# Gated linear attention before a mixture of experts: loads of a step issued singly, one product and one copy on other engines, state products ahead of the gate

## The chip, the cores and the metric

The kernel runs on one core of a Trainium2 chip. The metric is the device time of that core in microseconds (us), as the median of several executions. A core has five engines that run their own instruction streams and wait for each other through semaphores: TensorE (PE in the profile, with PEld for its weight loads), VectorE (DVE), ScalarE (ACT), GpSimd (POOL) and SyncE (SP). SyncE computes nothing here: it issues the DMAs between device memory and the on-chip memory, in the order of its stream. The profile also names queues: SPq is SyncE's.

## The reference

A recurrence over 768 positions for 4 batches and 8 heads of width 48, whose output is reshaped to 3072 tokens of width 384, followed by 8 experts with 384 tokens each:

```python
f = 1.0 / (1.0 + np.exp(-f_logit))
for t in range(S):
    state = f[:, :, t, :, None] * state + np.einsum('bhd,bhe->bhde', k[:, :, t], v[:, :, t])
    y[:, :, t] = np.einsum('bhd,bhde->bhe', q[:, :, t], state)
...
x = np.ascontiguousarray(attn_out.transpose(0, 2, 1, 3)).reshape(B * S, H * D)
logits = x @ w_gate
# pairs (token, expert) in falling order of logit; a token goes to the first expert with room
for e in range(E):
    mask = assigned == e
    h = np.maximum(x[mask] @ w1[e], 0.0)
    out[mask] = h @ w2[e]
```

All data are float32.

## The kernel before

The kernel has two parts, one behind the other on the same core. The first is the scan, which computes the recurrence and the gate's logits. The second finds the assignment of tokens to experts by a search (small VectorE and TensorE operations in alternation), gathers the tokens' rows from device memory, and runs the two matmuls of each expert. The change touches the scan alone.

The scan works on chunks of 128 positions of one batch with all 8 heads: 6 chunk positions times 4 batches are 24 chunks, numbered position first (`chunks`, line 357). A chunk goes through some thirty small functions, the stages. They are written out by hand as a tuple `stages` (line 358): each entry is a function and a number n, and step s calls the function on chunk s - n. So one step holds work of five chunks at different ages, and the tuple's order is the order of the instructions on every engine's stream; nothing is reordered later. `begun` is the order of the first three steps, -1 to 1 (line 363), `drain` and `finale` those of the last two. An entry `(None, 0)` is the place at which small jobs that prepare the search are put in ("extras" below).

What the stages do, by the names that the profile shows:

- `clamp` (line 164, GpSimd) and `decays` (169 and 170, ScalarE, two activations) turn the loaded `f` into the log-decay `g`.
- `cumulated` (174, TensorE) sums g over positions into the PSUM bank `L`; `clipped` (179, VectorE) reads it into `dl`; `powers` (185, ScalarE) makes `ek` and `eq`, exponentials of dl and of -dl.
- `scaled` (191) multiplies: `kg` = k * ek on GpSimd, `qg` = q * eq on VectorE.
- In the step after that, `turn_q` and `turn_k` (231, TensorE) transpose qg and kg into the two PSUM banks `T`; ScalarE copies them out (239). `products` (252, TensorE) multiplies kg with v for the new state, in a part of the PSUM bank `small`; `next_state` (263, VectorE) adds it to the faded old state `R`. `turned` (160, GpSimd) makes `w`, a copy of v's upper heads with the two halves of its positions exchanged. `scores` (273, TensorE) multiplies kT and qT.
- One step later, `masked0` and `masked1` (281, VectorE) copy the scores under the causal mask; `inner` (303) and `outer` (314), both TensorE, make the output in two PSUM banks `Y`.
- One step later still, `joined` adds the two banks (322 on ScalarE, then 323 on VectorE) into `yT`; `turn_y` (328, TensorE) transposes it into the first bank T; `copy_y` (334) copies it out as `x`, on VectorE for all but the last three chunks and on ScalarE for these; `gate` (344, TensorE) multiplies yT with the gate's weights `wg_rows` into columns of the bank L; `gated` (348, VectorE) takes the logits; `with_logits` (351, GpSimd) appends them to x; `store` (355, SyncE) writes x to device memory.
- `lengths` and `spanned` (204 on TensorE, 209 on VectorE), `faded` (217, ScalarE) and `kept_part` (223, GpSimd) make `R`; `gl` lies between (212, GpSimd).

The loads: `load` (line 141) is called at the head of step s for chunk s + 2 and puts four DMAs next to each other on SyncE's queue: q and k of that chunk, f of the chunk after it, and v. The tiles of f, k and q have 5 buffers each, v has 7 (`NV`). In front of the first step, chunks 0 and 1 are loaded in the same way; `load_gate` loads wg_rows at step 1.

The lines of the order that the change touches:

```python
(copy_k, 1), (cumulated, 0), (clipped, 0), (masked1, 2), (turn_y, 3), (copy_y, 3),
(gate, 3), (gated, 3), (decays, -1), (products, 1), (lengths, 0), (turned, 1),
(powers, 0), (scaled, 0), (spanned, 0), (next_state, 1), (faded, 0), (kept_part, 0),
```

Of the kernel before, what the change touches and what calls it, by code (L numbers as in the profile page):

```python
# [11 lines left out]
FP32 = mybir.dt.float32  # L12
# [3 lines left out]
ALU = mybir.AluOpType  # L16
# [9 lines left out]
def kernel(  # L26
# [11 lines left out]
    nc = tc.nc  # L38

    B, H, S, DH = q.shape  # L40
# [3 lines left out]
    C = 128  # L44
# [41 lines left out]
    work = attn.enter_context(tc.tile_pool(name="attn", bufs=2))  # L86

    def kept(shape, dtype, name):
        return work.tile(shape, dtype, name=name, tag=name, bufs=1)
# [6 lines left out]
    q_bufs = [kept([128, H, DP], FP32, f"qg{i}") for i in range(NB)]  # L96
    k_bufs = [kept([128, H, DP], FP32, f"kg{i}") for i in range(NB)]
    a_bufs = [kept([128, 2, HP, 128], FP32, f"am{i}") for i in range(NB)]
    NV = 7
    v_bufs = [kept([128, H, DP], FP32, f"v{i}") for i in range(NV)]  # L100
# [37 lines left out]

    state = {}

    def load(G):
        n = G["i"] + 1
        fetch(G, (("q", q), ("k", k)) if G["i"] else (("f", f_logit), ("k", k), ("q", q)))
        if n < len(chunks):
            fetch(chunks[n], (("f", f_logit),))
        fetch(G, (("v", v),))

    def fetch(G, parts):
        b, c = G["b"], G["c"]
        for nm, src in parts:  # L150
            t = v_bufs[G["i"] % NV] if nm == "v" else work.tile(
                [128, H, DH], FP32, name=nm, tag=nm, bufs=5)
            nc.sync.dma_start(
                out=t[:, :, 0:DH], in_=src[b, :, C * c:C * c + C, :].rearrange("h t d -> t h d"))
            G[nm] = t

    def turned(G):
        G["w"] = w = work.tile([128, H // 2, DP], FP32, name="w", tag="w", bufs=4)
# [27 lines left out]

    def scaled(G):
        i = G["i"] % NB
        for nm, t, src, e, eng in (("kg", k_bufs[i], "k", "ek", nc.gpsimd),
                                   ("qg", q_bufs[i], "q", "eq", nc.vector)):  # L190
            eng.tensor_tensor(out=t[:, :, 0:DH], in0=G[src][:], in1=G[e][:], op=ALU.mult)  # L191
            G[nm] = t


# [32 lines left out]
    def turn_of(nm, src):  # L227
        def turn(G):
            G[nm + "_ps"] = t = T[nm == "kT"]
            for hp in range(HP):  # L230
                nc.tensor.transpose(  # L231
                    out=t[:, 128 * hp:128 * hp + 128],
                    in_=G[src][:, 2 * hp:2 * hp + 2, :].rearrange("t h d -> t (h d)"),
                    identity=ident[:])

        def copy(G):
            G[nm] = work.tile([128, HP, 128], FP32, name=nm, tag=nm, bufs=3)
            to = G[nm][:].rearrange("p a t -> p (a t)")
            nc.scalar.copy(out=to, in_=G[nm + "_ps"][:])

        return turn, copy

    turn_k, copy_k = turn_of("kT", "kg")
# [86 lines left out]

    def copy_y(G):
        G["x"] = x = work.tile([128, DX], FP32, name="x", tag="x", bufs=5)
        copy = nc.scalar.copy if G["i"] + 3 >= len(chunks) else nc.vector.tensor_copy
        copy(
            out=x[:, 0:D].rearrange("t (a r b d) -> t a r b d", a=2, r=2, b=2),
            in_=G["X"][:].rearrange("t (a b r d) -> t a r b d", a=2, b=2, r=2)[:, :, :, :, 0:DH])

# [15 lines left out]
    def store(G):  # L353
# [2 lines left out]

    chunks = [{"b": b, "c": c, "i": c * B + b} for c in range(NCH) for b in range(B)]
    stages = ((clamp, -1), (masked0, 2), (joined, 3), (turn_q, 1), (copy_q, 1), (turn_k, 1),
              (copy_k, 1), (cumulated, 0), (clipped, 0), (masked1, 2), (turn_y, 3), (copy_y, 3),
              (gate, 3), (gated, 3), (decays, -1), (products, 1), (lengths, 0), (turned, 1),  # L360
              (powers, 0), (scaled, 0), (spanned, 0), (next_state, 1), (faded, 0), (kept_part, 0),
              (None, 0), (with_logits, 3), (scores, 1), (inner, 2), (outer, 2), (store, 3))
    begun = tuple(x for x in stages if x[1] >= 0) + ((clamp, -1), (decays, -1))
    drain = ((masked0, 2), (masked1, 2), (turn_q, 1), (joined, 3), (copy_q, 1), (turn_k, 1),
             (copy_k, 1), (turned, 1), (gate, 3), (gated, 3), (scores, 1), (None, 0), (turn_y, 3), (copy_y, 3),
             (inner, 2), (outer, 2), (masked0, 1), (masked1, 1), (None, 1), (with_logits, 3),
             (store, 3))
    finale = ((joined, 3), (inner, 2), (outer, 2), (None, 0), (gate, 3), (gated, 3), (turn_y, 3),
              (None, 1), (joined, 2), (copy_y, 3), (None, 2), (gate, 2), (gated, 2), (None, 3),
              (turn_y, 2), (copy_y, 2), (with_logits, 3), (store, 3), (with_logits, 2),  # L370
              (store, 2), (None, 4))
# [2 lines left out]
    def later(step, go, at=0):  # L374
        extras.setdefault((step, at), []).append(go)

    AHEAD = 2
    ALL = len(chunks) + 2

    def attention(first, last):  # L380
        for step in range(first, last):
            if AHEAD <= step + AHEAD < len(chunks):
                load(chunks[step + AHEAD])
            order = stages
            if step < 2:
                order = begun
            elif step > len(chunks):
                order = finale
            elif step == len(chunks):
                order = drain  # L390
            for stage, n in order:
                if stage is None:
                    for go in extras.pop((step, n), ()):
                        go()
                elif 0 <= step - n < len(chunks):
                    stage(chunks[step - n])
# [28 lines left out]
    def last_of(t, n):  # L425
        return t.unsqueeze(len(t.shape)).to_broadcast(tuple(t.shape) + (n,))
# [38 lines left out]
    for i in range(3):  # L465
        rows_ = slice(NQ * i // 3, NQ * (i + 1) // 3)
        later(11 + i, lambda r=rows_: nc.vector.tensor_copy(
            out=blocks[:, r], in_=last_of(linef[:, r], NT)))
# [84 lines left out]
    def load_weights(e, pool, slot, parts=(0, 1), behind=None):  # L553
        for part in parts:
            shape, src = (([128, DC, F], moe_w1), ([128, FC, D], moe_w2))[part]
            w = pool.tile(shape, FP32, name=f"w{part + 1}", tag=f"w{part + 1}_{slot}", bufs=1)
            if behind is not None:
                nc.scalar.copy(out=w[0:1, 0, 0:1], in_=behind)
            nc.sync.dma_start(out=w[:], in_=src[e].rearrange("(c p) f -> p c f", p=128))
            slots.setdefault(e, [None, None])[part] = w  # L560
# [29 lines left out]
    def load_gate():  # L590
# [9 lines left out]
        out=wg[:], in_=moe_w_gate.rearrange("(c p) e -> p c e", p=128)))  # L600
    later(0, lambda: idle_turns(5))
    with tc.manual_schedule(engines=FIXED):
        load(chunks[0])
        load(chunks[1])
        for z in range(2):
            nc.sync.dma_start(out=mask[HC * z:HC * z + HC, 1], in_=mask[HC - HC * z:C - HC * z, 0])
        attention(-1, LAST + 2)
        load_weights(0, early, 0)
        attention(LAST + 2, ALL)
        load_weights(1, early, 1)  # L610
# [765 lines left out]
    with tc.If(again > 0):  # L1376
# [7 lines left out]
        with tc.For_i(0, B, 1) as b:  # L1384
            x = pool.tile([128, NCH, D], FP32, name="xb", tag="xb", bufs=1)
            with tc.For_i(0, HP, 1) as hp:
                scan_pair(pool, x, b, hp)
            nc.sync.dma_start(
                out=xd[:, :].rearrange("(b c t) d -> b t c d", b=B, c=NCH)[
                    bass.ds(b, 1), :, :, 0:D].rearrange("b t c d -> (b t) c d"),  # L1390
                in_=x[:])
            for c in range(NCH):
                G = {"x": x[:, c, :]}
                X = ps("X", "T")
                for d in range(DC):
                    nc.tensor.transpose(out=X[:, 128 * d:128 * d + 128],
                                        in_=G["x"][:, 128 * d:128 * d + 128], identity=ident[:])
# [3 lines left out]
                for d in range(DC):  # L1401
# [3 lines left out]
                    out=logits[:, bass.ds(b * NCH + c, 1)].rearrange("p o e -> p (o e)"),  # L1405
                    in_=G["lg"])
# [30 lines left out]
```

## Time and profile before

| what | value |
|---|---|
| device time, median of 3 runs | 453.06 us (451.3 to 453.6) |
| the profiled execution | 454.26 us |
| its span in the profile | 452.5 us |
| mean granted TensorE clock | 0.981 |
| start of turn_q in steps 1 to 4 | 9.14, 14.20, 19.59, 25.55 us |
| start of turn_q in steps 5 to 9 | 30.93, 36.32, 42.49, 48.97, 56.01 us |
| start of turn_q in steps 12 to 15 | 73.49, 79.31, 85.15, 90.97 us |
| start of turn_q in steps 16 to 19 | 97.78, 104.77, 112.95, 119.37 us |
| start of turn_q in steps 21 to 23 | 131.02, 136.58, 142.25 us |
| first matmul of the experts | 179.5 us |

The span runs from the first to the last instruction of the profiled execution. The stretches from one turn_q to the next are the lengths of the steps: 5.8 us in the middle of the scan, more around 42 to 56 us and around 97 to 119 us. Busy times of the engines in four stretches, with the granted clock of TensorE and the share of time in which the DMA engines were busy:

```profile
core 0: us, PE busy (x) PEld busy (x) DVE busy (x) ACT busy (x) POOL busy (x), PEclk, DMA share, GB/s
31.00:41.80 10.80, 10.40 (x261) 9.01 (x261) 9.32 (x22) 7.27 (x16) 6.34 (x16) 1.00 0.95 206
79.30:85.10 5.80, 5.62 (x146) 4.78 (x142) 4.61 (x14) 3.61 (x8) 3.07 (x8) 1.00 0.85 180
104.80:113.00 8.20, 6.88 (x146) 5.68 (x143) 5.09 (x13) 3.60 (x8) 3.48 (x8) 0.87 0.70 152
113.00:119.40 6.40, 6.19 (x145) 5.43 (x143) 4.50 (x9) 3.73 (x8) 1.72 (x4) 0.90 0.62 118
```

The DMAs of the scan, with the size of one and the median time from issue to landing:

```profile
xd<-x SPq DMA_DIRECT2D x24, 196.0 KB, 2.2
f<-in_f_logit_dram SPq DMA_DIRECT2D x24, 192.0 KB, 3.7
k<-in_k_dram SPq DMA_DIRECT2D x24, 192.0 KB, 3.7
q<-in_q_dram SPq DMA_DIRECT2D x24, 192.0 KB, 3.3
v<-in_v_dram SPq DMA_DIRECT2D x24, 192.0 KB, 4.5
```

In the lines of a timeline, the columns are: start in us, length in us, engine, line of the kernel, operation, tile written <- tiles read, shape, number of instructions merged, and in brackets the idle time of the engine before it with the instruction that ended it. A matmul of a float32 operand appears as two records for each instruction of the program.

### The profile page before, as it was taken

How to read it: one execution, taken by the hardware profiler on the slowest of the kernel's cores; microseconds unless marked ns; L12 is line 12 of the kernel's file. 1: busy time of each engine (PE TensorE's matmuls, PEld its weight loads, DVE VectorE, ACT ScalarE, POOL GpSimd, SP SyncE). 2: the span in 40 equal slices, each digit the busy share in tenths (PEclk: the TensorE clock that was granted, in tenths of full speed). 3: DMA queues.
4: the chain of work that ended last, by engine and by line, in shares of the span. 5: the costliest groups of instructions: out<-in, count | busy, mean ns of one | idle time of the engine just before them, and what ended most of it. 6: DMA issues, size and time to landing. Idle time of an engine off the chain costs nothing.

```text
span 452.5 us, 11264 instructions
## 1 busy us (share of the span) xinstructions
PE 423.2 (94%) x4743; PEld 311.6 (69%) x4743; DVE 187.5 (41%) x608; ACT 151.4 (33%) x350; POOL 129.6 (29%) x230
## 2 busy tenths in 40 slices
PE   7899899998999868999999999999999999999992
PEld 3688788876888735868685858688887556556551
DVE  5688788876789764166666661000000000000000
ACT  4666466663665300312131212133323212212200
POOL 6455545554355105720000105001103203101010
PEclk9999999998999959999999999999999999999998
DMA  8799878885681593755444003049942201100000
GB/s 165 142 207 199 195 160 173 176 174 126 141 171 42 192 387 90 235 207 166 148 162 153 19 17 109 17 156 296 300 156 73 71 17 40 50 17 36 0 31 26
DMA packets 119148, 59.33 MB, mean 131 GB/s; under 512 B 102320, under 2 KB 113712, under 8 KB 119088
## 3 DMA queue, kind: packets, MB, share of 16 engines
q1 hardware_dynamic: 115824, 48.96, 41.0%
q0 software_dynamic: 3264, 9.56, 6.6%
q8 instruction: 39, 0.64, 0.6%
q14 instruction: 21, 0.17, 0.1%
HBM read 48.91 MB, written 9.54 MB: 129 GB/s over the span
## 4 chain that ended last, share of the span: by engine, by line
PE 72%; issue 15%; DVE 6%; POOL 3%; ACT 1%; POOLq 0%; ACTq 0%
PE H L665 22%; PE O L679 21%; PE T L231 5%; PE A L273 4%; PE Y L303 4%; PE L L174 3%; PE L L344 3%; DVE dl L179 3%; PE Y L314 2%; PE small L204 2%; PE small L252 2%; PE Xe L654 1%; POOL out_dram L685 1%; PE nothing L106 1%; PE cnt L778 1%
## 5 line engine op out<-in xcount | busy, mean ns | idle before, releaser
L679 PE MATMUL O<-w,hT 128*128 128x384 f32 x384 | 132.6, 490 | 0.0
L665 PE MATMUL H<-xeT,w 128*128 128x256 f32 (+2 forms) x624 | 130.7, 366 | 0.7 <-ACT xeT L657 0.7
L665 PEld LDWEIGHTS H<-xeT,w 128*128 128x128 f32 x624 | 99.2, 191 | 27.0 <-ACT xeT L657 1.0
L679 PEld LDWEIGHTS O<-w,hT 128*128 128x128 f32 x384 | 69.8, 190 | 39.1 <-issue 0.2
L685 POOL DMA_INDIRECT out_dram<-o,tok x24 | 23.3, 971 | 211.0 <-ACT o L684 205.6
L669 ACT ACTIVATE hT<-H 128x256 f32<-128x256 f32 (+2 forms) x104 | 38.2, 367 | 88.4 <-PE H L665 86.5
L191 POOL TENSOR_TENSOR kg<-k,ek 128x384 f32<-128x384 f32 x24 | 24.1, 1003 | 47.3 <-issue 46.9
L684 ACT COPY o<-O 128x384 f32<-128x384 f32 x24 | 11.5, 478 | 74.5 <-PE O L679 73.0
L281 DVE COPY_PREDICATED am<-mask,A 128x512 f32<-128x512 int32 x48 | 34.6, 725 | 0.9 <-PE A L273 0.9
L657 ACT COPY xeT<-Xe 128x384 f32<-128x384 f32 x24 | 11.4, 479 | 61.4 <-PE Xe L654 61.4
L718 POOL DMA_INDIRECT xe<-xd,tok x24 | 23.1, 963 | 23.5 <-DVE numb L407 16.5
L191 DVE TENSOR_TENSOR qg<-q,eq 128x384 f32<-128x384 f32 x24 | 26.4, 1101 | 4.7 <-ACT eq L185 2.6
L303 PE MATMUL Y<-am,v 64*64 64x128 f32 (+1 forms) x368 | 21.0, 247 | 2.4 <-issue 2.4
L323 DVE TENSOR_TENSOR yT<-Y,yT 128x512 f32<-128x512 f32 x23 | 15.9, 689 | 15.6 <-ACT yT L322 15.4
L273 PE MATMUL A<-qT,kT 48*64 48x128 f32 (+1 forms) x768 | 22.1, 251 | 0.0
L303 PE MATMUL Y<-am,w 64*64 64x128 f32 (+1 forms) x368 | 20.7, 249 | 0.9 <-issue 0.9
L322 ACT COPY yT<-Y 128x512 f32<-128x512 f32 x23 | 13.5, 586 | 22.7 <-PE Y L314 18.7
L174 PE MATMUL L<-g,wcum 128*128 128x384 f32 x48 | 19.7, 493 | 0.7 <-ACT g L170 0.7
L303 PEld LDWEIGHTS Y<-am,v 64*64 64x64 f32 x368 | 18.4, 136 | 2.6 <-issue 2.6
L160 POOL COPY w<-v 64x256 f32<-64x256 f32 x48 | 18.9, 394 | 2.5
L273 PEld LDWEIGHTS A<-qT,kT 48*64 48x64 f32 x768 | 18.5, 133 | 0.6
L303 PEld LDWEIGHTS Y<-am,w 64*64 64x64 f32 x368 | 17.6, 136 | 1.5 <-issue 1.5
(219 smaller groups left out, 531.3 us busy)
## 6 DMA issues: line engine op xcount, KB each, us to landing
w<-in_moe_w_dram SPq DMA_DIRECT2D x16, 1536.0 KB, 8.3
xd<-x SPq DMA_DIRECT2D x24, 196.0 KB, 2.2
f<-in_f_logit_dram SPq DMA_DIRECT2D x24, 192.0 KB, 3.7
k<-in_k_dram SPq DMA_DIRECT2D x24, 192.0 KB, 3.7
q<-in_q_dram SPq DMA_DIRECT2D x24, 192.0 KB, 3.3
v<-in_v_dram SPq DMA_DIRECT2D x24, 192.0 KB, 4.5
xe<-xd,tok POOLq DMA_INDIRECT x24, 3.4
out_dram<-o,tok POOLq DMA_INDIRECT x24, 2.6
```

The costliest lines, as they stand in the source:

```text
L160: nc.gpsimd.tensor_copy(out=w[HC * z:HC * z + HC], in_=G["v"][HC - HC * z:C - HC * z, H // 2:H])
L174: nc.tensor.matmul(out=G["Lv"], lhsT=wcum[:], rhs=g_bufs[G["i"] % NB][:, :, 0:DH], start=True, stop=True)
L191: eng.tensor_tensor(out=t[:, :, 0:DH], in0=G[src][:], in1=G[e][:], op=ALU.mult)
L231: nc.tensor.transpose(out=t[:, 128 * hp:128 * hp + 128], in_=G[src][:, 2 * hp:2 * hp + 2, :].rearrange("t h d -> t (h d)"), identity=ident[:])
L273: nc.tensor.matmul(out=A[par][to, 128 * hp + first * j:128 * hp + 128], lhsT=G["kT"][rows, hp, HC * j:HC * j + HC], rhs=G["qT"][rows, hp, ...
L281: nc.vector.copy_predicated(am[:, par].rearrange("s (a b) t -> s a b t", b=2), mask[:].unsqueeze(2).to_broadcast((128, 2, 2, 128)), A[par] ...
L303: nc.tensor.matmul(out=G["Y"][r0][DP * r:DP * r + DP, 128 * blk + first:128 * blk + 128], lhsT=v, rhs=G["am"][rows, h % 2, h // 2, first:128],
L665: nc.tensor.matmul(out=L["H"][:, 0:w], lhsT=slots[e][0][:, d, 128 * ft:128 * ft + 128], rhs=xT[:, d, 0:w], start=(d == 0), stop=(d == DC - 1))
L669: nc.scalar.activation(out=hT[:, ft, 0:w], in_=L["H"][:, 0:w], func=AF.Relu)
L679: nc.tensor.matmul(out=L["O"][:, 0:D], lhsT=hT[:, ft, 128 * i:128 * i + 128], rhs=slots[e][1][:, ft, :], start=(ft == 0), stop=(ft == FC - 1))
L685: nc.gpsimd.indirect_dma_start(out=outs[next(tiles)][:, :], out_offset=bass.IndirectOffsetOnAxis(ap=token(e, first_block + i), axis=0), in ...
L718: nc.gpsimd.indirect_dma_start(out=t[:], out_offset=None, in_=xd[:, :], in_offset=bass.IndirectOffsetOnAxis(ap=token(e, i), axis=0))
```

## The change

There are four edits. `load` is split into four stages, one for each input, and these stand inside the order of the step: f for four chunks ahead behind the `decays` of the step, v for three chunks ahead next to it, k and q for three chunks ahead behind `scaled`; their tiles have 3 buffers in place of 5. `scaled` puts both products on VectorE, kg first. `copy_y` is on ScalarE for every chunk and stands behind `powers`. `products` stands in front of `gate`, and `decays` moves ahead of both.

```diff
-    def load(G):
-        n = G["i"] + 1
-        fetch(G, (("q", q), ("k", k)) if G["i"] else (("f", f_logit), ("k", k), ("q", q)))
-        if n < len(chunks):
-            fetch(chunks[n], (("f", f_logit),))
-        fetch(G, (("v", v),))
-
-    def fetch(G, parts):
-        b, c = G["b"], G["c"]
-        for nm, src in parts:
-            t = v_bufs[G["i"] % NV] if nm == "v" else work.tile(
-                [128, H, DH], FP32, name=nm, tag=nm, bufs=5)
+    def load_of(nm, src):
+        def load(G):
+            G[nm] = t = v_bufs[G["i"] % NV] if nm == "v" else work.tile(
+                [128, H, DH], FP32, name=nm, tag=nm, bufs=3)
+            t0 = C * G["c"]
             nc.sync.dma_start(
-                out=t[:, :, 0:DH], in_=src[b, :, C * c:C * c + C, :].rearrange("h t d -> t h d"))
-            G[nm] = t
+                out=t[:, :, 0:DH], in_=src[G["b"], :, t0:t0 + C, :].rearrange("h t d -> t h d"))
+
+        return load
+
+    load_f, load_k, load_q, load_v = (
+        load_of(nm, src) for nm, src in (("f", f_logit), ("k", k), ("q", q), ("v", v)))
...
     def scaled(G):
         i = G["i"] % NB
-        for nm, t, src, e, eng in (("kg", k_bufs[i], "k", "ek", nc.gpsimd),
-                                   ("qg", q_bufs[i], "q", "eq", nc.vector)):
-            eng.tensor_tensor(out=t[:, :, 0:DH], in0=G[src][:], in1=G[e][:], op=ALU.mult)
+        for nm, t, src, e in (("kg", k_bufs[i], "k", "ek"), ("qg", q_bufs[i], "q", "eq")):
+            nc.vector.tensor_tensor(out=t[:, :, 0:DH], in0=G[src][:], in1=G[e][:], op=ALU.mult)
             G[nm] = t
...
     def copy_y(G):
         G["x"] = x = work.tile([128, DX], FP32, name="x", tag="x", bufs=5)
-        copy = nc.scalar.copy if G["i"] + 3 >= len(chunks) else nc.vector.tensor_copy
-        copy(
+        nc.scalar.copy(
...
-              (copy_k, 1), (cumulated, 0), (clipped, 0), (masked1, 2), (turn_y, 3), (copy_y, 3),
-              (gate, 3), (gated, 3), (decays, -1), (products, 1), (lengths, 0), (turned, 1),
-              (powers, 0), (scaled, 0), (spanned, 0), (next_state, 1), (faded, 0), (kept_part, 0),
-              (None, 0), (with_logits, 3), (scores, 1), (inner, 2), (outer, 2), (store, 3))
-    begun = tuple(x for x in stages if x[1] >= 0) + ((clamp, -1), (decays, -1))
+              (copy_k, 1), (cumulated, 0), (clipped, 0), (masked1, 2), (turn_y, 3), (decays, -1), (load_f, -4), (load_v, -3), (products, 1), (gate, 3), (gated, 3),
+              (lengths, 0), (turned, 1), (powers, 0), (copy_y, 3), (scaled, 0), (load_k, -3), (load_q, -3),
+              (spanned, 0), (next_state, 1), (faded, 0), (kept_part, 0), (None, 0),
+              (with_logits, 3), (scores, 1), (inner, 2), (outer, 2), (store, 3))
+    begun = tuple(x for x in stages if x[1] >= 0) + tuple(x for x in stages if x[1] < 0)
...
-    AHEAD = 2
...
-            if AHEAD <= step + AHEAD < len(chunks):
-                load(chunks[step + AHEAD])
...
-        load(chunks[0])
-        load(chunks[1])
+        for load, n in ((load_f, 0), (load_k, 0), (load_q, 0), (load_f, 1), (load_v, 0), (load_k, 1),
+                        (load_q, 1), (load_f, 2), (load_v, 1)):
+            load(chunks[n])
```

## The prediction

> **What bounds the kernel now.** I read the page's engine totals first, then the chain that ended last, then the waits of TensorE, then the timeline of one step engine by engine.
>
> ```profile
> PE 423.2 (94%) x4743; PEld 311.6 (69%) x4743; DVE 187.5 (41%) x608; ACT 151.4 (33%) x350; POOL 129.6 (29%) x230
> ...
> PE 72%; issue 15%; DVE 6%; POOL 3%; ACT 1%; POOLq 0%; ACTq 0%
> ```
>
> TensorE is busy 94% of the span and carries the chain. The scan (the part the change touches) runs to about 157 us, one step every 5.83 us in the undisturbed stretch; behind it come a search and the experts' matmuls, which the diff leaves alone. So the question is how much earlier the scan ends. One step on TensorE, matmuls (start, length, last bracket: idle before):
>
> ```profile
> 79.31 0.66 PE L231 MATMUL T<-ident,qg 128*128 128x128 f32 x4
> 79.81 0.60 PE L231 MATMUL T<-ident,kg 128*128 128x128 f32 x4
> 80.25 0.81 PE L174 MATMUL L<-g,wcum 128*128 128x384 f32 x2
> 80.91 0.63 PE L328 MATMUL T<-ident,yT 128*128 128x128 f32 x4
> 81.71 0.64 PE L344 MATMUL L<-wg_rows,yT 128*64 128x8 f32 x16 [0.18 <-DVE dl L179]
> 82.20 0.65 PE L252 MATMUL small<-v,kg 128*64 128x48 f32 x16
> 82.68 0.60 PE L204 MATMUL small<-ind,g 128*64 128x2 f32 x16
> 83.21 0.90 PE L273 MATMUL A<-qT,kT 48*64 48x128 f32 x32
> ```
>
> Read the distances between starts, since lengths overlap. Four transposes take 0.44 us (79.81 to 80.25), but from the transposes of yT to the gate it is 0.80. The gate stands still 0.36 us, not the 0.18 shown, until VectorE has read L into dl (ends 81.66). It is the only standing wait of the step. The rest of the step is scores, inner and outer, until 85.15.
>
> The same step on VectorE and GpSimd:
>
> ```profile
> 81.10 0.56 DVE L179 TENSOR_SCALAR dl<-L 128x384 f32<-128x384 f32 x1 [0.34 <-PE L L174]
> 81.57 0.73 DVE L281 COPY_PREDICATED am<-mask,A 128x512 f32<-128x512 int32 x1
> 82.19 0.54 DVE L334 COPY x<-T 128x384 f32<-128x384 f32 x1
> 82.66 0.15 DVE L348 COPY logits<-L 128x8 f32<-128x8 f32 x1
> 82.92 1.11 DVE L191 TENSOR_TENSOR qg<-q,eq 128x384 f32<-128x384 f32 x1
> ...
> 82.61 1.00 POOL L191 TENSOR_TENSOR kg<-k,ek 128x384 f32<-128x384 f32 x1 [1.74 <-issue]
> ```
>
> qg starts 0.31 us after kg and ends 0.42 us after kg ends (84.03 against 83.61). The first step shows the same (9.00 against 8.58), and so does the third (19.53 against 19.12). A length that follows another engine's end looks like a lock: about 0.4 of qg's 1.11 us are its own.
>
> [...] From the stall at 96.64 us to the one at 103.16 I count 128 matmuls and as many weight loads, 256 in all. [...]
>
> **The change, part by part.** Times are relative to turn_q's start (79.31 is 0).
>
> *Products ahead of the gate.* The products need kg and v of an earlier chunk, ready long before. They run 2.04 to 2.52 (1.60 + 0.44, then the 0.48 between rows L252 and L204). dl ends at 2.35, so the gate starts at 2.52 without waiting, 0.17 spare. The step falls from 5.83 to 5.47. Next to be late is turn_y itself: yT ends at 1.45 and its transposes start at 1.60, which is when L's two matmuls end too. That tie stays as it is. If dl came over 0.17 later, the wait would return. Steps that have both gate and products: 4 to 20, 17 of them (step 3 goes to the start, and the last 4 chunks have no products). 17 x 0.36 = 6.1 us.
>
> *kg on VectorE.* GpSimd loses 1.00 us; VectorE gains one product. With GpSimd idle at that time (turned ends at 1.56, gl starts after spans at 4.6) neither product is blocked. Cost of one: at best 0.42 (the remainder above), at worst 1.11 (the row taken whole). I take 0.5: the 0.42 and a start. Logits can be read at 3.20 (gate at 2.52 plus 0.68, the distance in the step at 22.55), ek is there at 3.17, so kg runs 3.3 to 3.8 and qg 3.8 to 4.3 (eq is there at 3.58). Today qg ends at 4.72. The next turn_q wants it at 5.47: 1.1 us spare. Behind qg queue spans, st, the extras and masked0, and masked0 waits anyway for the scores, which now end near 4.4. VectorE per step: -0.54 (x) - 1.11 + 1.0 = 0.65 less.
>
> *x's copy on ScalarE.* +0.48 us per step (the L334 ACT row: 478 ns). ScalarE is busy 3.61 of 5.8 us in this step, then 4.1 of 5.47. It stands after eq, 3.5 to 4.0; behind it are gl (GpSimd feeds it near 4.6) and the yT copy (next step, 0.14). T is free at 4.0, wanted at 5.47. Nothing on the path.
>
> *Loads.* A step issues f, v, k and q separately, f for four chunks on, the others for three. As built, f waits on ScalarE (g done, 2.75), k and q on VectorE (3.8 and 4.3), v on TensorE's reads of four steps ago. These waits sit on SP, in front of the step's other loads and the store of x. SP needs 0.43 to 0.9 us per load, 0.36 for the store: about 2.8 of 5.47. f and k land 3.7 us after issue (page) and are used near three steps, 15 us, later: 11 us spare. Bandwidth: 4 x 192 + 196 = 964 KB per 5.47 us is 176 GB/s; the stretch 31.0 to 41.8 us moved 206 at a DMA share of 0.95. Taken as nothing. From the other side: late loads would show as waits at clamp or kg, and a step at full DMA share would be 964 KB / 217 GB/s = 4.4 us, so bandwidth cannot set 5.47.
>
> *The start.* Steps 0 to 3 run on latency. In step 0 kg and qg end at 8.55 instead of 9.00; clamp of chunk 1 no longer queues behind kg on GpSimd (8.55), nor do its decays, so they are done by 9.0 instead of 10.47. turn_q then starts at 8.6 (9.14 before), L follows at 9.65 (10.53), next turn_q at 12.8 (14.20), the next at 17.2 (19.59): 2.4 us. k and q of chunk 2 are issued about 2 us later than now, near 11 to 12 us, land by 16 at the 3.3 to 3.7 us of the page, and are wanted at 16.1: no spare, up to 0.5 us lost. The step from 19.59 waits 0.69 us at its gate, where I read the landing of wg_rows (issued 17.4 to 19.8, median 3.0 us); the change issues these after the same number of loads but the step comes sooner, so that wait may grow to 1.2. I take 2.3 us, with 0 and 3.4 as bounds.
>
> *Sum.* 6.1 + 2.3 = 8.4 us. The profiled execution took 454.26 us (span 452.5), 1.2 above the median of 453.06. 454.26 - 8.4 = 445.9 profiled; 444.7 as a median. Not priced: the fetch gaps (the steps around them are longer than 5.83 by 0.3, 0.6, 1.2, 1.0, 1.2 and 1.2 us, 5.5 in sum) and the reduced clock of 105 to 119 us (0.87 and 0.90; 1.8 us of longer steps). [...] No row tells the sign; both could vanish or double.
>
> **Rivals.**
> A. As summed: 444.7, own range 442 to 448.
> B. Fetch gaps shrink because loads leave in single pieces: 5.5 us more, 439. For it: gaps come in two clusters, so their surroundings matter. [...]
> C. The gain at the gate is real but swallowed: the start gains nothing (k and q of chunk 2 and wg_rows late) and the fetch gaps grow by their own 5.5 us: 454.26 - 6.1 + 5.5 = 453.7 profiled, 452.5 as a median. Against: loads have 11 us of slack from step 4 on.
> D. Slower. kg and qg cost 1.05 each even alone, one after the other. They end at 5.4, spans, st and 0.4 us of extras end at 6.15, masked0 at 6.8, where today yT starts at 6.23 (0.76 of the next step). turn_y slips and the loop closes over VectorE: about 5.9 us per step, 17 x 0.07 = +1.2 us, and +1.8 at the start (three links 0.6 longer each): 457.3 profiled, 456 as a median. It decides once a product takes over 0.8 us (two from 3.3 must end by 4.86). Against it: the 0.42 us remainder, the same in every step that I read.
>
> **How the numbers follow.** A 0.64, B 0.14, C 0.12, D 0.10. The forecast is A's 444.7. The range 440 to 450 holds A, its unpriced fetch gaps on either side and the upper part of B; most of C and D, near 2 in 10, stay outside. What this kernel's measurements can tell from no change is 0.5%, 2.3 us. Faster (below 450.8): A, B and a little of C, 0.81. Within: most of C, 0.10. Slower (above 455.3): 0.09.
>
> **What would show it.** Right: the gate row without a wait on dl and the products row before it; turn_q every 5.47 us; kg and qg on VectorE near 0.5 us each; copy_y on ScalarE near 0.48; the scan's end some 8 us sooner with everything behind it shifted alike. Wrong: products near 1.1 us (D), clamp or kg waiting on a DMA (C), "issue" gaps in the scan far from 5.5 us, a longer wait of the first gate on wg_rows, or a search that starts earlier yet experts that do not.

## The result and the profile after

| | before | changed |
|---|---|---|
| device time, median of 20 executions each | 451.87 us (451.1 to 453.6) | 448.39 us (445.3 to 451.76) |
| ratio to before, 95% interval | | 0.9924 (0.9903 to 0.9945) |
| the profiled execution, its span | 454.26 us, 452.5 us | 447.81 us, 446.0 us |

The change makes the kernel 3.5 us faster. The prediction's 444.7 us stood against a median of 453.06 from three runs, a gain of 8.4 us. So the direction was right and the size 2.4 times too large. That 448.39 us lies between the 440 and 450 that the prediction gave is luck: this range was drawn for the unpriced issue gaps, and not for what happened. (Issue gaps are idle times of TensorE that the profile puts down to "issue", in the profile before 0.89, 0.72, 0.91 and 1.17 us in front of 54.98, 97.36, 104.06 and 111.05 us. The prediction calls them fetch gaps; that instruction fetches make them was the author's estimate, and no run shows it.) With twenty runs the kernel before is at 451.87 us; its profiled execution, on which the sum was made, was slower than all of these, so the 6.5 us between the two spans overstate the gain.

The engine totals and the chain of the changed kernel:

```profile
PE 421.9 (95%) x4743; PEld 312.2 (70%) x4743; DVE 176.6 (40%) x611; ACT 159.1 (36%) x371; POOL 107.0 (24%) x206
...
PE 76%; issue 14%; DVE 4%; POOL 2%; ACT 1%; DMA 1%; SPq 0%; POOLq 0%; ACTq 0%; DVEq 0%
```

VectorE is busy 10.9 us less although it has taken over kg, GpSimd 22.6 us less, ScalarE 7.7 us more. TensorE does the same work and still carries the chain. New in it is 1% of DMA: a chain that waits for a transfer.

One step on TensorE, and the products on VectorE in it (start and length in us):

```profile
77.99 0.66 PE L227 MATMUL T<-ident,qg 128*128 128x128 f32 x4
78.48 0.60 PE L227 MATMUL T<-ident,kg 128*128 128x128 f32 x4
78.92 0.81 PE L171 MATMUL L<-g,wcum 128*128 128x384 f32 x2
79.59 0.63 PE L324 MATMUL T<-ident,yT 128*128 128x128 f32 x4
80.15 0.67 PE L248 MATMUL small<-v,kg 128*64 128x48 f32 x16
80.65 0.60 PE L339 MATMUL L<-wg_rows,yT 128*64 128x8 f32 x16
81.10 0.61 PE L200 MATMUL small<-ind,g 128*64 128x2 f32 x16
...
83.58 0.66 PE L227 MATMUL T<-ident,qg 128*128 128x128 f32 x4
```

```profile
81.30 0.17 DVE L343 COPY logits<-L 128x8 f32<-128x8 f32 x1 [0.33 <-PE L L339]
81.38 0.56 DVE L187 TENSOR_TENSOR kg<-k,ek 128x384 f32<-128x384 f32 x1
81.86 0.55 DVE L187 TENSOR_TENSOR qg<-q,eq 128x384 f32<-128x384 f32 x1
```

The gate's wait on dl is gone, and both products take 0.56 us in the place of 1.00 and 1.11. But the step is 5.59 us, not 5.47. From the transposes of yT to the products it is 0.56 us, where four transposes take 0.44 (78.48 to 78.92): 0.12 us are left between them that no wait explains. (The rows count one record for each transpose, so x4 is four of them; the one product of L171 is x2.)

Then the start. Before, the first gate and the loads of wg_rows that it needs stood like this:

```profile
22.55 0.64 PE L344 MATMUL L<-wg_rows,yT 128*64 128x8 f32 x16 [0.69 <-DVE am L281]
```

```profile
17.36 2.44 SPq L593 DMA_DIRECT2D wg_rows<-in_moe_w_gate_dram  x4
```

The bracket names a VectorE instruction that ended at this moment, but the gate does not read its result; the last of the four loads, issued at 19.4 us, took 3.2 us and landed at the same moment, 22.6 us. In the changed kernel, the first gate on TensorE, the DMA queue's loads of wg_rows, and who waits (waits: engine and line that waited, what it waited for, us in total, times, longest):

```profile
19.17 0.62 PE L324 MATMUL T<-ident,yT 128*128 128x128 f32 x4
19.72 0.67 PE L248 MATMUL small<-v,kg 128*64 128x48 f32 x16
21.90 0.64 PE L339 MATMUL L<-wg_rows,yT 128*64 128x8 f32 x16 [1.50 <-DMA wg_rows<-in_moe_w_gate_dram]
22.36 0.64 PE L200 MATMUL small<-ind,g 128*64 128x2 f32 x16
22.93 1.56 PE L269 MATMUL A<-qT,kT 48*64 48x128 f32 x32
25.70 0.94 PE L227 MATMUL T<-ident,qg 128*128 128x128 f32 x4
```

```profile
17.55 2.98 SPq L585 DMA_DIRECT2D wg_rows<-in_moe_w_gate_dram  x4
```

```profile
PE L L339 <- DMA wg_rows<-in_moe_w_gate_dram: 1.5, 1, 1.5
```

The step from 17.60 to 25.70 us lasts 8.1 us. The gate stands 1.5 us for wg_rows. Behind it the scores, 0.90 us long in an undisturbed step, take 1.56. The granted clock explains that; windows of the changed kernel around it (columns as in the table of stretches above: span, busy times, PEclk, DMA share, GB/s):

```profile
19.00:22.00 3.00, 1.50 (x26) 1.10 (x25) 1.22 (x3) 2.50 (x6) 0.35 (x2) 1.00 0.26 37
22.00:24.00 2.00, 2.00 (x56) 1.98 (x60) 1.42 (x5) 0.00 (x0) 0.94 (x2) 0.73 1.15 223
24.00:26.00 2.00, 2.00 (x50) 1.88 (x43) 0.96 (x3) 0.19 (x1) 0.91 (x3) 0.50 1.04 205
26.00:28.00 2.00, 2.00 (x14) 1.61 (x12) 0.93 (x2) 1.72 (x4) 0.00 (x0) 0.92 0.96 191
```

After the standstill TensorE runs at half its clock (0.50); the 1.7 us of full clock that these windows lack (2 x 0.27 + 2 x 0.50 + 2 x 0.08) are 3.4 us at half. Note also the DMA share of 0.26 from 19 to 22 us, around the end of the 2.98 us in which four small loads of 3 KB hold the queue. The kernel before has 0.26 in this window too, and run 1 below, where these loads are issued from 13.14 us on, 0.85.

Where the two profiles stand, by the start of turn_q (us):

| step | 1 | 2 | 3 | 4 | 9 | 15 | 20 | 24 |
|---|---|---|---|---|---|---|---|---|
| before | 9.14 | 14.20 | 19.59 | 25.55 | 56.01 | 90.97 | 125.20 | 147.61 |
| changed | 9.09 | 13.07 | 17.60 | 25.70 | 55.64 | 89.17 | 119.18 | 141.35 |

At step 3 the changed kernel is 2.0 us ahead, at step 4 it is 0.15 behind. From step 9 to 15 it gains 0.24 us a step. From 15 to 20 it gains 4.2 us, where five steps of 0.24 would give 1.2, because this one execution of the kernel before had issue gaps of 0.72, 0.91 and 1.17 us and a clock of 0.87 and 0.90 there.

### The profile page after: what moved, and what is told of

Read it like the earlier page. It is cut to its first block, busy times and chain, and to the rows that moved or that the text cites. A ratio compares the mean times of both kernels' runs of the same rounds, so it can differ in the third digit from the quotient of the medians.

```text
span 446.0 us, 11315 instructions
## 1 busy us (share of the span) xinstructions
PE 421.9 (95%) x4743; PEld 312.2 (70%) x4743; DVE 176.6 (40%) x611; ACT 159.1 (36%) x371; POOL 107.0 (24%) x206
## 4 chain that ended last, share of the span: by engine, by line
PE 76%; issue 14%; DVE 4%; POOL 2%; ACT 1%; DMA 1%; SPq 0%; POOLq 0%; ACTq 0%; DVEq 0%
PE H L658 22%; PE O L672 21%; PE T L227 5%; PE A L269 4%; PE Y L299 4%; PE L L171 3%; PE small L248 2%; PE L L339 2%; PE small L200 2%; PE T L324 2%; PE Y L310 2%; PE Xe L647 1%; POOL out_dram L678 1%; PE nothing L106 1%; PE T L106 1%
## 5 line engine op out<-in xcount | busy, mean ns | idle before, releaser
L319 DVE TENSOR_TENSOR yT<-Y,yT 128x512 f32<-128x512 f32 x23 | 15.9, 691 | 17.3 <-ACT yT L318 17.2
L208 POOL TENSOR_TENSOR gl<-spans 128x4 f32<-128x4 f32 x20 | 4.9, 246 | 66.8 <-PE A L269 42.7
L157 POOL COPY w<-v 64x256 f32<-64x256 f32 x48 | 19.4, 405 | 2.8 <-DMA v<-in_v_dram 0.3
L171 PE MATMUL L<-g,wcum 128*128 128x384 f32 x48 | 19.6, 490 | 0.0
L176 DVE TENSOR_SCALAR dl<-L 128x384 f32<-128x384 f32 x24 | 13.4, 558 | 11.2 <-PE L L171 11.2
```

The source lines that it names most:

```text
L157: nc.gpsimd.tensor_copy(out=w[HC * z:HC * z + HC], in_=G["v"][HC - HC * z:C - HC * z, H // 2:H])
L171: nc.tensor.matmul(out=G["Lv"], lhsT=wcum[:], rhs=g_bufs[G["i"] % NB][:, :, 0:DH], start=True, stop=True)
L319: nc.vector.tensor_tensor(out=flat, in0=G["Y"][0][:], in1=flat, op=ALU.add)
```

## The experiments

Ratios are to the kernel before, run on the same chip in the same set, and stand as they are on record; they can differ from the quotient of the two medians, in run 1 (0.9888) and run 2 (0.9924) by 0.003. Runs 5 to 8 fell on a chip on which everything took some 11 us longer (before: 462.86 us), so times are compared through ratios. The theory that was tested, S: the gate's real wait was 0.25 us a step, and the products' place is the whole gain of the steps; the start gains 2 us by kg on VectorE and earlier loads, and loses them at the first gate to wg_rows and to the clock. Rivals are named with each run.

**1. wg_rows earlier.**

```diff
-    later(1, load_gate)
+    later(0, load_gate)
```

> The changed kernel with the four loads of wg_rows issued in step 0 instead of step 1. Theory S (the start lost its gain because the first gate waited for wg_rows, 1.7 us, and TensorE then ran 1.3 us longer on a reduced clock): wg_rows is issued near 13 us, lands before 19 us, the wait at the first gate is gone, turn_q of step 4 starts near 22.7 us instead of 25.7, and the time falls by about 3 us against the changed kernel (448.4 to 445.4; ratio to before 0.986). Rival D (the start is bound by the DMA engines as a whole, so what is issued later is late in its turn): the f, v, k, q behind wg_rows come 2 to 3 us later, clamp or kg waits for them, and turn_q of step 4 stays near 25.5 us; time as the changed kernel, ratio 0.992.

Measured: 0.9859 (0.9831 to 0.9887), 446.95 us; the changed kernel's interval lies above. turn_q of step 4 starts at 23.80 us. The wait for wg_rows is gone and the clock stays at 1.00, but a smaller wait took its place:

```profile
23.80 0.63 PE L227 MATMUL T<-ident,qg 128*128 128x128 f32 x4 [0.68 <-ACT yT L318]
```

S holds, at 1.9 us in place of 3 in the profile. D may have a part: f of chunk 4 is now issued behind wg_rows, at 16.45 us, and if it arrives late, so are ScalarE's decays and what stands behind them (run 6 tests this).

**2. The products' place alone.**

```diff
-              (gate, 3), (gated, 3), (decays, -1), (products, 1), (lengths, 0), (turned, 1),
+              (products, 1), (gate, 3), (gated, 3), (decays, -1), (lengths, 0), (turned, 1),
```

> The kernel before with one edit: the state products stand in front of the gate. Theory S (the gate's real wait was 0.25 us a step, 0.11 of the 0.36 that I read being a price of going over from transposes to matmuls of 64 columns): the distance from turn_y to the products is 0.55 us, the step is 5.58 us, 17 steps gain 4.2 us, ratio 0.991. The sum of the prediction would give a step of 5.47 and 6.1 us, ratio 0.986. Rival V (VectorE sets the step once the gate no longer waits, so kg's move and x's copy are needed too): step stays near 5.8, ratio 0.998 or more.

Measured: 0.9898 (0.9875 to 0.9922), 448.61 us. The undisturbed steps are 5.58 to 5.59 us. On TensorE:

```profile
62.99 0.63 PE L328 MATMUL T<-ident,yT 128*128 128x128 f32 x4
63.55 0.67 PE L252 MATMUL small<-v,kg 128*64 128x48 f32 x16
64.05 0.60 PE L344 MATMUL L<-wg_rows,yT 128*64 128x8 f32 x16
```

The distance from the transposes to the products is 0.56 us here too, with kg on GpSimd and the old loads. This edit alone gives what the whole change gives (runs 10 and 11 repeat the comparison on one chip). It helps the start too: the products fill the time in which the first gate waited for wg_rows, and step 3 takes 5.29 us in place of 5.96. V falls: VectorE does not set the step without the other edits.

**3. All but the products' place.**

```diff
...
-(products, 1), (gate, 3), (gated, 3),
+(gate, 3), (gated, 3), (products, 1),
...
```

> The changed kernel with the gate put back in front of the products, all else as changed. If the products' place carries the gain of the steps: step back to 5.83 us, 4.2 us more than the changed kernel, ratio to before near 1.001 (the start's gain being lost to wg_rows). If the other edits carry some of it (rival): step between 5.58 and 5.83, ratio below 0.997.

Measured: 1.0007 (0.9983 to 1.0032), 452.2 us; steps of 5.82 to 5.83 us with the wait on dl back at every gate. The other three edits together give nothing that can be measured. The wait for wg_rows is 2.0 us here, and the granted clock is 0.50 from 22 to 28 us; step 3 takes 9.61 us.

**4. Another filler in front of the gate.** The lengths take the place of the products, in the kernel before.

```diff
-              (gate, 3), (gated, 3), (decays, -1), (products, 1), (lengths, 0), (turned, 1),
+              (lengths, 0), (gate, 3), (gated, 3), (decays, -1), (products, 1), (turned, 1),
```

> The kernel before with the lengths (not the products) in front of the gate; nothing else. They need g alone, which is done long before. If the 0.11 us belongs to going over from the transposes to 64-column matmuls, turn_y to lengths is 0.55 us as well and the step 5.58 us. If it is a wait of the products' own (for v, kg or the bank), turn_y to lengths is 0.44 us and the step 5.47 us.

Measured: 0.9899 (0.9869 to 0.9929).

```profile
62.69 0.63 PE L328 MATMUL T<-ident,yT 128*128 128x128 f32 x4
63.25 0.63 PE L204 MATMUL small<-ind,g 128*64 128x2 f32 x16
63.74 0.62 PE L344 MATMUL L<-wg_rows,yT 128*64 128x8 f32 x16
```

0.56 us again, with matmuls that need nothing but a long finished g. The 0.12 us belong to going over from the transposes to matmuls that write 64 columns (128*64 in the rows), and to no wait of the products. What TensorE does in them the runs don't show. The step is 5.62 us, 0.04 more than with the products.

**5. kg on VectorE alone**, in the kernel before (the edit of `scaled` as in the change).

> The kernel before with one edit: both products of scaled on VectorE, kg first. Theory S (the products cost 0.55 us each, the start gains 2 us by it and loses it at the first gate): turn_q of steps 1 to 3 starts at about 9.0, 13.1 and 17.6 us, the first gate waits for wg_rows until about 21.9 us, turn_q of step 4 starts at 25.5 us or later, and the steps stay at 5.83 us; ratio 0.998 to 1.004. Rival R (kg on VectorE brings the start its 2 us in this kernel, and it is the new loads that lose it): turn_q of step 4 near 23 us and ratio near 0.995.

Measured: 0.9993 (0.9971 to 1.0016). turn_q of steps 1 to 4: 9.05, 13.03, 19.20, 25.05 us; steps of 5.83. Nothing in the steps, as S has it; but the start lost its gain one step sooner than I expected, in step 2, before wg_rows was wanted at all. TensorE stands 1.57 us in front of turn_q of step 3:

```profile
19.20 0.66 PE L230 MATMUL T<-ident,qg 128*128 128x128 f32 x4 [1.57 <-DVE qg L190]
```

**6. wg_rows behind f of chunk 4**, in step 0 of the changed kernel (`begun` gets a stage behind load_f that calls load_gate once; `later(1, load_gate)` goes).

> The changed kernel with the loads of wg_rows issued in step 0, directly behind f of chunk 4 and in front of v, k and q of chunk 3. In the run with wg_rows at the head of step 0's loads a wait of 0.68 us was left in front of turn_q of step 4, since that f came late. Theory S: both waits go, turn_q of step 4 starts near 23.0 us, 0.7 us less than that run (446.3, ratio 0.985). Rival D (the DMA engines are the bound): v, k or q of chunk 3 are late instead, kg waits for its k, turn_q of step 4 near 24 us, same time as that run.

Measured: 0.9874 (0.9835 to 0.9912). turn_q of step 4 starts at 23.41 us and TensorE waits for nothing in that step. turn_q of step 4 is 0.4 us earlier than in run 1, although this profile's scan began 0.2 us later: step 3 takes 5.26 us in place of 5.87, nearly what S said. The time is not better: the issue gaps of this profile are larger (1.11, 1.19 and 1.12 us, in three steps of 7.0 us near 34 to 55 us). The two placings of wg_rows can't be told apart in time.

**7. The old loads**, all else as changed (`load` and `fetch` of the kernel before, called at the head of a step, 5 buffers).

> The changed kernel with its loads undone: four at the head of a step, for two chunks on, 5 buffers, as before; kg on VectorE, x's copy on ScalarE and the products' place as changed. Theory S (the new loads neither gain nor lose): step 5.58 us, first gate waits for wg_rows, time as the changed kernel within 1.5 us, ratio 0.990 to 0.995. Rival R (issuing singly costs by itself, through wg_rows or through the fetch gaps): faster than the changed kernel by 2 us or more, ratio below 0.989; if it gains, ratio above 0.996.

Measured: 0.9944 (0.9922 to 0.9966), as with the new loads. Here turn_q of steps 1 to 4 starts at 8.89, 12.87, 19.28 and 25.85 us. The waits of GpSimd and VectorE in the start, and kg of chunk 2 on VectorE:

```profile
POOL f L164 <- DMA f<-in_f_logit_dram: 7.6, 3, 5.5
DVE kg L190 <- ACT ek L185: 3.5, 3, 2.4
```

```profile
18.20 0.56 DVE L190 TENSOR_TENSOR kg<-k,ek 128x384 f32<-128x384 f32 x1 [2.36 <-ACT ek L185]
```

Theory S was right on the steps (5.58 us) and the time, but not on the start: the first gate waits for nothing here. The time is lost before it. TensorE stands 1.83 us for qg in front of step 3, and the granted clock is 0.50 from 19 to 22 us, so steps 2 and 3 take 6.41 and 6.57 us.

This is what run 5 ran into. The old order issues f of chunk 3 behind q and k of chunk 2; clamp waits for it, the decays stand in front of ek on ScalarE, and kg waits 2.4 us (2.1 in run 5). The new order issues that f first, and step 2 is 4.53 us in place of 6.41. But the place in the queue is not all of it. The clamp of chunk 3, here and in the kernel before:

```profile
16.14 0.51 POOL L164 TENSOR_SCALAR f<-f 128x384 f32<-128x384 f32 x1 [5.55 <-DMA f<-in_f_logit_dram]
```

```profile
14.73 0.51 POOL L164 TENSOR_SCALAR f<-f 128x384 f32<-128x384 f32 x1 [0.22 <-DMA f<-in_f_logit_dram]
```

In both this f is issued at the same time (11.07 and 11.01 us), and here it lands 1.4 us later; why, the runs don't show. So the new loads have a use, in the start, but only together with kg on VectorE (in run 9, with kg on GpSimd, steps 1 and 2 take 5.05 and 5.39 us with the new loads, as before), and wg_rows takes it away one step later.

**8. TensorE kept busy while it waits.**

```diff
+    def warm(G):
+        if G["i"] == 0:
+            for _ in range(7):
+                nc.tensor.matmul(out=T[1][:, 0:3 * 128], lhsT=ones16[:], rhs=idle[:],
+                                 start=True, stop=True)
...
-(products, 1), (gate, 3), (gated, 3),
+(products, 1), (warm, 3), (gate, 3), (gated, 3),
...
```

> The changed kernel with 7 idle matmuls (128x384, 16 bit) of no use to the result, once, between the products and the gate of chunk 0, where TensorE stands 1.5 us for wg_rows. The wait is left as it is. If the loss behind that wait comes from the clock that falls while TensorE stands (theory C), the granted clock stays 1.00 from 22 to 28 us, turn_q of step 4 starts near 24.3 us instead of 25.7 and the time falls by 1.4 us. If the slow matmuls behind the wait have another cause (the DMA traffic of that moment, late masks), turn_q of step 4 stays at 25.7 us.

Measured: turn_q of step 4 at 24.64 us in place of 25.70, with the gate still waiting 0.2 us for wg_rows behind the filler. The gate and the windows:

```profile
22.11 0.64 PE L339 MATMUL L<-wg_rows,yT 128*64 128x8 f32 x16 [0.25 <-DMA wg_rows<-in_moe_w_gate_dram]
```

```profile
22.00:24.00 2.00, 1.89 (x72) 1.90 (x76) 1.21 (x5) 0.00 (x0) 0.87 (x2) 1.00 1.09 213
24.00:26.00 2.00, 2.00 (x46) 1.70 (x37) 1.67 (x5) 1.25 (x3) 1.13 (x3) 1.00 1.17 233
```

The DMA traffic is as heavy as before (1.09 and 1.17) and the clock stays at 1.00. So here it was the standing still that lowered the clock, theory C. From the gate to turn_q of step 4 it is 2.53 us in place of 3.80 (21.90 to 25.70), so the low clock cost 1.3 us. This rests on one profile, and not every standstill of this length lowers the clock (last section). In time it can't be seen: 0.9927 (0.9895 to 0.9959); this profile had a step of 8.25 us near 50 us.

**9 to 12, on one chip.** kg back on GpSimd in the kernel of run 1; then the changed kernel, the products alone, and run 1, each once more.

> The changed kernel with wg_rows issued in step 0 (as in the run of that edit) and kg back on GpSimd. Theory S (kg on VectorE is worth about 1 us, at the start alone, and nothing in the steps): turn_q of steps 2 and 3 near 14.2 and 19.6 us instead of 13.4 and 17.9, of step 4 near 24.7 instead of 23.8, steps 5.58 us; ratio 0.988 to 0.990 against 0.986 with kg on VectorE. Rival R (a product blocked on VectorE costs the steps too): steps above 5.7 us and ratio above 0.992.

> The changed kernel once more, beside the next two on one chip: ratio to before 0.990 to 0.9945 as measured first.

> The kernel before with the products in front of the gate alone, once more: if this edit is the whole net gain of the change, its ratio lies within 0.003 of the changed kernel's in this row of runs; if the other edits gave something by themselves it is above by more, if they lost something below by more.

> The changed kernel with wg_rows issued in step 0, once more: 2 to 3 us below the changed kernel on the same chip, ratio 0.985 to 0.988.

| kernel | ratio, 95% interval | turn_q of step 4 | undisturbed step |
|---|---|---|---|
| 10, as changed | 0.9934 (0.9910 to 0.9957) | 26.14 us | 5.58 us |
| 11, products' place alone | 0.9933 (0.9912 to 0.9954) | 25.98 us | 5.58 us |
| 12, changed, wg_rows in step 0 | 0.9877 (0.9857 to 0.9898) | 23.96 us | 5.58 us |
| 9, as 12, kg on GpSimd | 0.9897 (0.9878 to 0.9917) | 25.58 us | 5.59 us |

In run 10 the gate waits 1.8 us for wg_rows and the low clock lasts into step 4, which takes 6.59 us. The changed kernel and the products alone are equal. With wg_rows in time the change is 2.6 us better (446.69 against 449.34 us), the fastest version of this study. kg on VectorE is then worth 1.6 us at step 4 by the profiles (1.3 counted from turn_q of step 1, at 9.60 and 9.93 us) and about 1 us in time (447.81 against 446.69, overlapping intervals), at the start alone; the steps stay as they are, and rival R of run 9 falls.

## Why the prediction was right and wrong

**What bounds the kernel** was right: TensorE's step in the scan, with the gate as the only standing wait. Everything behind the scan moved with it: the experts' first matmul starts at 173.2 us in place of 179.5. Of the 4.9 us by which the sum was too large, 2.0 are in the gate's term and 2.4 in the start's; the rest stays open.

**Products ahead of the gate: right in mechanism, mis-sized.** The step "The gate stands still 0.36 us" took the pace of transposes followed by another matmul of 128 columns as TensorE's own time, and called the rest a wait. Of the 0.36, 0.12 stay when the wait is gone (runs 2 and 4). 17 x 0.24 is 4.1 us, not 6.1. The gain of this edit alone is 4.6 us by the ratio of run 2 (0.9898; 3.4 us by its medians) and 3.0 us by that of run 11 (0.9933). The page's own figure, 0.18 idle, counts from the end that the profile gives the last transpose and was too small; 0.24 lies between.

**kg on VectorE: right.** The remainder of 0.42 us and a start gave 0.5; the products take 0.55 to 0.56. Rival D is refuted by that row. qg takes 0.55 us where no product runs on GpSimd, and 1.11 us beside kg there, ending 0.42 us after kg: the prediction's reading, that most of the 1.11 us was not its own, fits.

**x's copy: right**, 0.46 us on ScalarE and on no path.

**Loads: right for the steps, half seen for the start.** In run 7 the old loads gave the same time. That f of chunk 3 comes first turned out to carry step 2; I had looked only at k and q of chunk 2, which were not late.

**The start: this is the step that failed.** I wrote that the wait at the first gate "may grow to 1.2" and took 2.3 us of gain. The 2.0 us are there at step 3 (from steps 1 and 2; the half microsecond that I gave step 0 isn't, with turn_q at 9.09 against 9.14) and gone at step 4. wg_rows is issued at 17.55 us, no earlier than before (17.36): in every profile that leaves its place unchanged, the nineteen transfers in front of it hold SyncE's queue until 17.2 to 17.9 us. So an earlier gate only waits longer. And the wait has a price that I did not count: TensorE's clock falls to half (0.50) behind it. The step took 8.10 us, and 5.26 in run 6, where nothing was late. Of these 2.8 us, 1.7 are the wait (the gate at 21.90 where it could have started near 20.2) and 1.1 the clock, near the 1.3 that run 8 gave back. The longer wait of the first gate stood among the signs of being wrong, and rival C was nearest here: it said that the start gains nothing with wg_rows late, and was wrong in letting the issue gaps swallow the rest.

**Issue gaps: still open.** The excess of the disturbed steps over the normal one is 7.3 us in the profile before, 4.75 and 5.0 us in two profiles of the changed kernel, 4.7 and 7.6 us in two profiles of the products alone, 2.9 to 7.6 us over all runs. One profile for each run can't tell the loads' part from chance. The longest gap of the scan lasts 1.46 us (run 12, at 45 us). What makes the gaps is not shown: the page before lists an instruction queue (q8, 39 packets, 0.64 MB), but one of its packets also falls into the step from 79.3 to 85.1 us, which has no such gap, and no row shows a gap that waits for one.

**The sum, corrected:** 4.1 us for the gate, 0.15 lost at the start: 4 us, against 3.5 us measured, with an interval of 2.5 to 4.4. That they meet is in part luck. The loss at the start is read from one profile; in run 10, where the low clock lasted longer, turn_q of step 5 starts at 32.73 us against 30.93 before, and the 16 steps behind it (3.8 us) would leave 2 us.

## What to carry to other kernels

When work is pulled forward, list every transfer that the pulled instruction reads and ask whether its issue moves too; where the queue in front of a transfer stays as long as it was, an earlier consumer only waits longer (the first gate 1.50 us in place of 0.69). Measure a wait against the same pair of neighbours without the wait, not against the pace of one of them. A standstill of TensorE of one and a half to two microseconds was followed by a halved clock (0.50) in four of five profiles here. In a start it pays to remove its cause (runs 1 and 12); filling it kept the clock up, but showed no gain in time (run 8).

## What the runs showed of the hardware

**A standstill can halve the clock.** Standstills of TensorE of 1.5 us (changed kernel), 1.8 us (runs 7 and 10) and 2.0 us (run 3) in the start were followed by a granted clock of 0.50, and so was the issue gap of 1.17 us at 110 us before (0.50 from 111 to 114 us). But the length alone does not decide. Two standstills of 0.68 us (run 1) and 0.69 us (before) left the clock at 1.00, and so did the 1.57 us of run 5. Behind issue gaps of 1.40 us in run 2 and 1.46 us in run 12 four transposes took 0.44 and 0.43 us, the pace of an undisturbed step (0.44 us). The windows of run 5, then those of run 7:

```profile
19.00:22.00 3.00, 2.28 (x14) 1.54 (x14) 2.73 (x7) 2.08 (x5) 1.97 (x6) 1.00 0.34 54
22.00:24.00 2.00, 1.95 (x68) 1.96 (x72) 1.88 (x7) 0.76 (x2) 0.46 (x1) 1.00 1.04 205
```

```profile
19.00:22.00 3.00, 2.72 (x10) 2.33 (x11) 1.78 (x5) 1.35 (x4) 1.98 (x6) 0.50 0.38 61
22.00:24.00 2.00, 2.00 (x45) 1.51 (x43) 1.21 (x2) 1.70 (x5) 0.00 (x0) 0.92 1.02 201
```

What else decides it, the runs don't show. The half clock lasted 3.4 us in the changed kernel (worked out above), and as long behind the gap of 1.17 us before (windows of 1 us from 110 to 115 us: 0.90, 0.50, 0.50, 0.50, 0.89). Run 10's windows of 2, 2, 2 and 3 us at 0.60, 0.50, 0.50 and 0.80 lack 3.4 us of full clock, that is 6.8 us at half, twice as long.

**The clock goes with the spread.** The five fastest executions of the changed kernel (445.3 to 447.0 us) have a mean clock of 0.982 to 0.985, its five slowest (450.0 to 451.8 us) 0.966 to 0.977.

**A change of matmul form costs a little.** Going from the transposes to matmuls of 64 columns costs TensorE 0.12 us beyond the transposes' pace (0.56 in place of 0.44 us), for the products and the lengths alike (runs 2 and 4).
